# GpSimd casting loads for w_ch1, TensorE row broadcasts and a two-ring DMA model in a hand-planned attention and mixer kernel

## The chip, the cores and the metric

The kernel runs on one core of a Trainium2 chip. The metric is device time in microseconds (us): the median of five runs.

## The reference

Sliding-window attention with sinks over q, k, v of shape (4, 8, 768, 64) is followed by a residual mixer MLP over 512 features. All inputs and the output are float32.

```python
# attention, n_sink = 4, window = 128
scores = q @ k.T / sqrt(64)
keep = (pos_k < 4) | ((0 <= pos_q - pos_k) & (pos_q - pos_k < 128))
x = softmax(where(keep, scores, -1e9)) @ v          # -> (4, 768, 512)
# mixer
a1 = alpha1 * x + beta1
u = x + lam * einsum('ts,bsd->btd', w_tok, a1)       # w_tok 768 x 768
a2 = alpha2 * u + beta2
out = u + lam * (relu(a2 @ w_ch1) @ w_ch2)           # 512 x 2048, 2048 x 512
```

## The kernel before

All four batches (b = 0 to 3) run in one program. Every step is registered as a task with `add` (L51): a priority, the engines that could run it with a cost in ns for each, the function that emits the instruction, the tasks it comes after, the buffers it uses. `Plan.emit` (L63) is a list scheduler: it always takes the task that could start earliest by its own clock, and of those that tie the one with the lowest priority number; it chooses engine and buffer and emits the instruction. So the order in every engine's queue, SyncE's DMA queue among them, follows from the costs written into the source. A DMA lands in the planner's clock after one shared `channel` (L129 to L131): issue, 1600 ns, then the transfers one after the other by their `lands`. Buffers are named by kind with a fixed number of homes (L211): eight "nat" (q or k of a head pair), four "wst" (staging of 512 KB weight pieces), four "d" (one PSUM bank each), two "S" (two PSUM banks each).

Per batch: q and k are loaded in fp32, cast to fp16 (`n16`), transposed to `qkT` (batches 0 and 1 on TensorE with the tile `tp`, L431; later ones by DMA transposes, L445). `scores` (L500) multiplies them into `S`, ScalarE takes the exponential into `E` (L538), VectorE masks it (L547) or a bias matmul did (L518). `pv` (L555) multiplies by v (`vf`) and normalises into `x` (L593, L594). For batch 0 GpSimd multiplies each half of x by lam*alpha1 (`la1_b`) into `xh` (L603); for later batches it multiplies and adds lam*beta1 (`lb1_b`; L612, L615). `tok` (L692) is the token matmul with the transposed w_tok (`wtokT`), added to x (L710), giving u. u is cast (L226 or L228), transposed (batch 0 on TensorE, L745; later by DMA, L763), scaled (`affine`, L725), and goes through `mlp1` (h, L784, relu L790 or L792) and `mlp2` (ch, L808, added at L819, stored at L822). Work on batch b + 1's attention is planned among batch b's MLP.

What the change touches:

- w_ch1 (`load_w1`, L391): eight loads of 512 KB by SyncE into "wst" staging, then sixteen casts (`cast_w1`, L669) on ScalarE, GpSimd or VectorE into `w1f`. w_ch2 uses the same staging (`load_w2`, L396) and is multiplied by lam while it is cast (`cast_w2`, L678, into `w2f`).
- lam, alpha1, beta1: three one-partition rows are loaded by ScalarE's queue (L240). `spread` (L662) broadcasts a row over 128 partitions with an fp32 matmul by a row of ones; before, only lam*alpha1 goes that way. lam and beta1 are also loaded again by SyncE with a broadcast (`load_const`, L386, 256 KB each), and GpSimd multiplies them at full size (L859). A row of lam*beta1 in fp16 (`lb16`) serves batch 0's extra token matmul (L705).
- row sums of w_tok (`row`, L646): six matmuls per tile of `wtokT` by a matrix with one column of ones.
- idle matmuls (L217, L112): where the planner's TensorE has a gap before 14 us of its clock, it emits one 128-column matmul per 75 ns of gap, into one PSUM bank that is held back for it until 14.5 us (L215, L222).
- v of batch 0 (`cast_v0`, L628) goes to GpSimd or ScalarE.

Of the kernel before, what the change touches and what calls it, by code (L numbers as in the profile page):

```python
# [12 lines left out]

PE, ACT, DVE, POOL, SP = "pe", "act", "dve", "pool", "sp"
# [4 lines left out]
class Buf:  # L19


    def __init__(self, kind, shape, dtype, name):
        self.kind, self.shape, self.dtype, self.name = kind, shape, dtype, name
        self.left = 0
        self.freed = 0.0
        self.home = None
        self.t = None

# [11 lines left out]
class Plan:  # L40
# [10 lines left out]
    def add(self, prio, engs, fn, after=(), uses=(), mode=None, lands=0.0, port=False,  # L51
            since=0.0):

        t = Task(prio, engs, fn, after, uses, mode, lands, port)
        t.ready = max(t.ready, since)
        for b in uses:
            b.left += 1
        for a in t.needs:
            a.then.append(t)
        self.tasks.append(t)  # L60
        return t

    def emit(self):  # L63
# [3 lines left out]
        open_ = []  # L67

# [3 lines left out]
        for t in self.tasks:  # L72
            if not waiting[id(t)]:
                admit(t)
        free = {e: 0.0 for e in (PE, ACT, DVE, POOL, SP)}
        mode = None
        channel = 0.0
        port = 0.0
        done = 0
        while done < len(self.tasks):  # L80
# [20 lines left out]
            assert best is not None, "no task can go on"  # L101
# [11 lines left out]
            if e == PE and free[PE] < until:  # L113
                for _ in range(int((start - max(free[PE], 900.0)) / took)):
                    idle()
                    mode = None
            t.fn(e)
            cost = t.engs[e]
            if e == PE:
                if start < 4500.0:  # L120
                    cost = cost * 2
                if t.mode != mode:
                    cost = cost + 95
                mode = t.mode
# [4 lines left out]
            if e == SP:  # L129
                channel = max(channel, free[e] + 1600.0) + t.lands  # L130
                t.seen = channel + 300.0  # L131
            else:
                t.seen = free[e] + SEEN[e]
            for b in t.uses:
                b.left -= 1
                b.freed = max(b.freed, t.seen)
                if b.left == 0:
                    self.busy[b.kind][b.home] = False
                    self.homes[b.kind][b.home] = b.freed
            for o in t.then:  # L140
                o.ready = max(o.ready, t.seen)
                waiting[id(o)] -= 1
                if not waiting[id(o)]:
                    admit(o)
            done += 1
# [4 lines left out]
def kernel(  # L150
# [64 lines left out]
    idle_ps = ps.tile([P, 512], FP32, tag="d_3", bufs=1, name="idle")  # L215

    def idle():  # L217
        nc.tensor.matmul(idle_ps[:, 0:P], iden, iden, start=True, stop=True)

    plan = Plan(pools, homes, (14000.0, idle, 75.0))  # L220
    add = plan.add
    plan.homes["d"][3] = 14500.0  # L222
# [33 lines left out]
    ones_c = const.tile([P, P], FP16, name="ones_c")  # L256
    nc.vector.memset(ones_c, 0.0)
    nc.vector.memset(ones_c[:, 0:1], 1.0)
# [60 lines left out]


# [10 lines left out]
    def load_qk(p, b, hp, t, wait=None):  # L331
        bf = nat[b, hp, t] = Buf("nat", None, None, f"nat{b}_{hp}_{t}")
        src = (q, k)[t][b, 2 * hp : 2 * hp + 2]
        if b < XB:
            src = src.rearrange("h (p r) d -> p h (r d)", p=P)
            done["nat", b, hp, t] = add(
                p, {SP: 480}, lambda e: nc.sync.dma_start(bf.t, src), [wait], [bf], lands=1110)  # L337
        else:
            src = src.rearrange("h s d -> (h s) d").rearrange("(x p) d -> p x d", p=P)
            done["nat", b, hp, t] = add(  # L340
                p, {SP: 700}, lambda e: nc.sync.dma_start(
                    bf.t.rearrange("p e (r d) -> p (e r) d", r=NR), src), [wait], [bf], lands=1740)

    def load_v(p, b, r, wait=None):
        bf = vn[b, r] = Buf("vnat", None, None, f"vnat{b}_{r}")
        done["vn", b, r] = add(
            p, {SP: 550}, lambda e: nc.sync.dma_start(
                bf.t, v[b, :, r * P : (r + 1) * P, :].rearrange("h p d -> p h d")),
            [wait], [bf], lands=1150)
# [3 lines left out]
    def load_v0(p, G, r):  # L353
        if G == 0:
            if r == 0:
                v0[G, 0] = Buf("uT", [P, NR, 4, D], FP32, "v0_0")
            bf, sl = v0[G, 0], r
        else:
            if r % 3 == 0:
                v0[G, r // 3] = Buf("wst", [P, 3, 4, D], FP32, f"v0_1_{r // 3}")  # L360
            bf, sl = v0[G, r // 3], r % 3
        v0["at", G, r] = (bf, sl)
        done["v0", G, r] = add(
            p, {SP: 520}, lambda e: nc.sync.dma_start(  # L364
                bf.t[:, sl], v[0, 4 * G : 4 * G + 4, r * P : (r + 1) * P, :].rearrange("h p d -> p h d")),
            uses=[bf], lands=590)
# [3 lines left out]
    def load_wtok(p, ti):  # L370
        if ti % 3 == 0:
# [5 lines left out]
            uses=[bf], lands=1060)  # L377
# [3 lines left out]
    def load_w(p, key, src):  # L381
        bf = wst[key] = Buf("wst", None, None, f"wst_{key}")
        done["wst", key] = add(
            p, {SP: 400}, lambda e: nc.sync.dma_start(bf.t, src), uses=[bf], lands=1400)

    def load_const(p, name, tile_, src):  # L386
        done[name] = add(
            p, {SP: 500}, lambda e: nc.sync.dma_start(tile_, src.unsqueeze(0).to_broadcast([P, DM])),
            lands=850)

    def load_w1(p, i):  # L391
        for c in range(0, NC, 2):
            load_w(p + 0.1 * c, f"w1_{i}_{c}",
                   moe_w_ch1[c * P : (c + 2) * P, i * 512 : (i + 1) * 512].rearrange("(c p) f -> p c f", p=P))
# [16 lines left out]
    def trans(p, b, hp, t, engs, evac, cast_p=None, wait=None):  # L411
# [31 lines left out]
        if b >= XB:  # L443
# [4 lines left out]
                [a] + prior, [bn, o], lands=600)  # L448
# [179 lines left out]
    def cast_v0(p, G, r):  # L628
        bf, sl = v0["at", G, r]
        done["vf", 0, r, G] = add(  # L630
            p, ({POOL: 400, ACT: 408}, {POOL: 400})[G],
# [4 lines left out]
    def cast_wtok(p, ti):  # L636
# [3 lines left out]
        pr = Buf("d", [P, P], FP32, f"rs{ti}")  # L640

# [3 lines left out]

        def row(e):  # L646
            for si in range(NR):
                nc.tensor.matmul(
                    pr.t, ones_c, wtokT[:, si, ti * P : (ti + 1) * P],
                    start=(si == 0), stop=(si == NR - 1))  # L650

        a = add(p, {ACT: 831, POOL: 829}, lambda e: copy(e, w.t.rearrange("p r i -> p (r i)"), src.t[:, ti % 3, :]),
                [done["wtn", ti]], [src, w], port=True)
        a = add(p + 0.1, {PE: 330}, tr, [a], [w, pt])
# [3 lines left out]
        a = add(p + 0.3, {PE: 330}, row, [a], [pr])  # L658
# [3 lines left out]
    def spread(p, name, src, o):  # L662
# [3 lines left out]
                [done.get(name)], [pt], since=9000.0)  # L666
        done[name] = add(p + 0.1, {DVE: 600, ACT: 600}, lambda e: copy(e, o, pt.t), [a], [pt])

    def cast_w1(p, i):  # L669
        for c in range(NC):  # L670
            src = wst[f"w1_{i}_{c - c % 2}"]
            done["w1", i, c] = add(
                p, {ACT: 619, POOL: 618, DVE: 430},
                lambda e, c=c, src=src: copy(
                    e, w1f[:, c, i * 512 : (i + 1) * 512], src.t[:, c % 2, :]),
                [done["wst", f"w1_{i}_{c - c % 2}"]], [src], port=True)
# [80 lines left out]
    def uTx(p, b, ti):  # L757

        if (b, 0) not in uT:
# [5 lines left out]
            [done["u16", b, ti]], [bu, bo], lands=600)  # L765
# [3 lines left out]
        for c in range(NC):  # L769
            o = (c, slice(chk * NTOK, (chk + 1) * NTOK))  # L770
            done["uT", b, chk, c] = add(
                p + 0.1 + 0.01 * c, {DVE: 380, ACT: 500},
# [3 lines left out]
    def mlp1(p, b, chk, fi):  # L776
# [11 lines left out]
        def relu(e):  # L788
            if e == ACT:
                nc.scalar.activation(bh.t[:, fi, :], ph.t, AF.Relu)  # L790
            else:
# [3 lines left out]
                [done["uT", b, chk, c] for c in range(NC)] + [done["w1", fi // 4, c] for c in range(NC)],  # L795
# [3 lines left out]
    def mlp2(p, b, ti, part):  # L799
# [16 lines left out]
        if part == 3:  # L816
            def oa(e):
# [6 lines left out]
                [a], [bx], lands=800)  # L824


    t0 = -1000.0
    n = 0
# [17 lines left out]
    load_w1(at(), 0)  # L846
    load_const(at(), "lam", lam_b, moe_lam)
    load_const(t0 + 150, "b1", lb1_b, moe_beta1)
    for i in range(1, 4):
        load_w1(at(), i)  # L850

    def spread_rows():
        done["la1"] = add(-880, {POOL: 1270}, lambda e: nc.gpsimd.tensor_mul(rows[1], rows[1], rows[0]),
                          since=9000.0)
        spread(-879, "la1", rows[1], la1_b)
        a = add(-990, {POOL: 400}, lambda e: nc.gpsimd.memset(lb16.t, 0.0), [], [lb16])
        done["lb1"] = add(-879, {POOL: 1270}, lambda e: nc.gpsimd.tensor_mul(lb16.t[0:1], rows[2], rows[0]),
                          [a], [lb16], since=9000.0)
        done["lb1b"] = add(20, {POOL: 1270}, lambda e: nc.gpsimd.tensor_mul(lb1_b, lb1_b, lam_b),  # L859
                           [done["lam"], done["b1"]])  # L860
        pt = Buf("d", [P, 2 * NC], FP32, "abT")
        a = add(-850, {PE: 200}, lambda e: nc.tensor.transpose(pt.t, ab_row, iden8), [], [pt],
                since=9000.0)
# [12 lines left out]
    for G in range(2):  # L876
        base = -900 + 60 * G
        for j in range(NR):
            scores(base + 10 * j, 0, j, (G,), bias=G == 1 or j > 1)
# [6 lines left out]
    cast_w1(1.5, 0)  # L886
# [5 lines left out]
    for b in range(B):  # L892
# [17 lines left out]
        if b == 0:  # L910
            for i in range(1, 4):
                cast_w1(w0 + 8 + 8 * (i - 1) - 4, i)
# [13 lines left out]
        if b + 1 < B:  # L926
            nb = b + 1
            if nb >= XB:
                for i, (hp, t) in enumerate(QK_ORDER):
                    load_qk(w0 - 30 + i, nb, hp, t, done["qkT", b, 3, 1])  # L930
                for r in range(NR):
                    load_v(w0 - 20 + r, nb, r, done["qkT", b, 3, 1])
# [8 lines left out]
            for i, (what, *args) in enumerate(steps):  # L941
                p = w0 + lo + (hi - lo) * i / len(steps) + 0.5
                if what == "T":
                    hp, t = QK_ORDER[args[0]]
                    trans(p if nb < XB else w0 - 15 + i, nb, hp, t, {POOL: 829}, {DVE: 955, ACT: 800},
# [47 lines left out]
```

The softmax here doesn't subtract the row's maximum and nothing guards it: scores larger than these inputs give would overflow.

## Time and profile before

| | us |
|---|---|
| median of 5 runs | 274.21 |
| lowest, highest | 272.13, 276.47 |
| the profiled execution | 272.13 |
| its span | 270.4 |
| TensorE busy (share of the span) | 258.3 (96%) |
| VectorE, ScalarE, GpSimd busy | 142.7, 129.9, 116.5 |
| first batch-0 h matmul | 43.12 |
| last w2f multiply ends | 82.5 |

The span is what the profiler recorded of one execution, and all shares refer to it. TensorE's matmuls are pipelined and their ends are modelled: a 128-column matmul is shown with 219 ns although such matmuls follow each other much more closely, so a busy TensorE need not be at its peak, and a gap shorter than such an end is not shown. The granted TensorE clock is 1.00 in this run from start to end. "Idle before, releaser" names what an instruction waited for last.

### The profile page before, as it was taken

The numbers are of one execution on the slowest core, as the hardware profiler recorded it, in microseconds if no ns is written. First come the engines' busy times: TensorE is split into PE (matmuls) and PEld (weight loads), VectorE is DVE, ScalarE is ACT, GpSimd is POOL, SyncE is SP. The second block draws the span as 40 slices with busy tenths as digits, with TensorE's granted clock in tenths as the row PEclk, the third lists the DMA queues.
The fourth block names the chain that finished last, engine by engine and source line by source line (L and its number), as shares of the span: only waits on it lengthen the run. The fifth ranks groups of instructions, "written<-read, shape, count | busy, mean of one in ns | idle before, by whom it ended". The sixth has DMA issues, their size and how long they took to land.

```text
span 270.4 us, 4969 instructions
## 1 busy us (share of the span) xinstructions
PE 258.3 (96%) x1941; PEld 141.6 (52%) x1941; DVE 142.7 (53%) x292; ACT 129.9 (48%) x213; POOL 116.5 (43%) x139
## 2 busy tenths in 40 slices
PE   7889999997899999799999999999999999999994
PEld 7544746654454544356655444555654445565441
DVE  5465745678899925357884234378953343100222
ACT  2688836777842003789640025787600145773000
POOL 5579947820596793117988600005755000000000
PEclk9999999999999999999999999999999999999999
DMA  6999998999999736799967523200011232000222
GB/s 208 322 247 354 383 312 252 293 350 282 235 282 204 190 92 168 175 190 215 217 136 164 153 78 97 62 0 2 0 39 44 97 98 80 0 0 2 78 78 78
DMA packets 85838, 42.28 MB, mean 156 GB/s; under 512 B 73515, under 2 KB 77619, under 8 KB 85814
## 3 DMA queue, kind: packets, MB, share of 16 engines
q1 hardware_dynamic: 85792, 41.95, 58.0%
q8 instruction: 15, 0.25, 0.4%
q14 instruction: 9, 0.07, 0.1%
q10 hardware_dynamic: 22, 0.01, 0.0%
HBM read 30.16 MB, written 6.29 MB: 135 GB/s over the span
## 4 chain that ended last, share of the span: by engine, by line
PE 68%; DMA 16%; SPq 5%; DVE 5%; POOL 2%; issue 1%; ACT 1%; DVEq 0%; POOLq 0%; ACTq 0%
PE ch L808 29%; PE h L784 24%; PE tok L701 9%; DMA wst_w<-in_moe_w_ch_dram 8%; DMA nat<-in_q_dram 6%; SPq L364 3%; DMA lb_b<-in_moe_beta_dram 3%; DVE w2f L683 3%; PE pv L570 3%; PE S L523 2%; DVE E L547 1%; SPq L375 1%; PE pv L563 1%; POOL n L228 1%; SPq L337 1%
## 5 line engine op out<-in xcount | busy, mean ns | idle before, releaser
L784 PE MATMUL h<-uT,w1f 128*128 128x384 f16 x512 | 90.3, 326 | 2.9 <-DVE uT L730 1.5
L808 PE MATMUL ch<-w2f,hT 128*128 128x512 f16 x384 | 88.5, 379 | 0.2 <-DVE w2f L683 0.2
L784 PEld LDWEIGHTS <-w1f 128*128 128x128 f16 x512 | 47.7, 98 | 36.2 <-issue 7.1
L808 PEld LDWEIGHTS <-hT 128*128 128x128 f16 x384 | 36.3, 98 | 41.4 <-issue 0.9
L790 ACT ACTIVATE hT<-h 128x384 f16<-128x384 f32 x95 | 46.2, 493 | 18.7 <-PE h L784 17.0
L538 ACT ACTIVATE E<-S 128x1024 f16<-128x1024 f32 (+1 forms) x42 | 40.7, 1002 | 12.9 <-PE pv L570 8.2
L819 DVE TENSOR_TENSOR x<-x,ch 128x512 f32<-128x512 f32 x24 | 16.5, 686 | 52.2 <-PE ch L808 51.7
L612 POOL TENSOR_TENSOR tmp<-x,la_b 128x512 f32<-128x512 f32 x18 | 25.8, 1435 | 41.4 <-DVE x L594 39.1
L226 ACT CAST u<-x 128x512 f16<-128x512 f32 x20 | 12.3, 618 | 61.7 <-DVE x L710 61.7
L701 PE MATMUL tok<-xh,wtokT 128*128 128x512 f16 x144 | 34.4, 379 | 0.0
L228 POOL CAST n<-nat 128x768 f16<-128x768 f32 x28 | 25.9, 937 | 16.7 <-DMA nat<-in_q_dram 11.9
L710 DVE TENSOR_TENSOR x<-x,tok 128x512 f32<-128x512 f32 x24 | 16.4, 687 | 23.6 <-PE tok L701 18.6
L615 POOL TENSOR_TENSOR xh<-tmp,lb_b 128x512 f16<-128x512 f32 x18 | 25.4, 1414 | 0.7
L792 DVE TENSOR_SCALAR hT<-h 128x384 f16<-128x384 f32 x33 | 18.3, 554 | 10.6 <-PE h L784 10.3
L547 DVE TENSOR_TENSOR E<-E,maskn 128x1024 f16<-128x1024 f16 x25 | 23.7, 977 | 0.0
L701 PEld LDWEIGHTS <-wtokT 128*128 128x128 f16 x144 | 13.9, 98 | 16.1
L594 DVE TENSOR_TENSOR x<-pv,rec 128x256 f32<-128x256 f32 x48 | 20.4, 424 | 1.7
L570 PE MATMUL pv<-vf,E 128*128 128x65 f16 x328 | 18.1, 194 | 2.3 <-DVE E L547 1.1
L570 PEld LDWEIGHTS <-E 128*128 128x128 f16 x328 | 15.3, 97 | 8.4 <-DVE E L547 1.8
L228 POOL CAST vf<-vnat 128x512 f16<-128x512 f32 x18 | 10.8, 618 | 9.3 <-PE h L784 7.1
L683 DVE TENSOR_TENSOR w2f<-wst_w,lam_b 128x512 f16<-128x512 f32 x15 | 12.6, 878 | 3.5 <-DMA wst_w<-in_moe_w_ch_dram 3.5
L228 POOL CAST u<-x 128x512 f16<-128x512 f32 x4 | 2.5, 629 | 26.3 <-DVE x L710 26.3
(94 smaller groups left out, 202.5 us busy)
## 6 DMA issues: line engine op xcount, KB each, us to landing
wst_w<-in_moe_w_ch_dram SPq DMA_DIRECT2D x16, 512.0 KB, 7.5
nat<-in_q_dram SPq DMA_DIRECT2D x16, 384.0 KB, 5.7
nat<-in_k_dram SPq DMA_DIRECT2D x16, 384.0 KB, 8.2
out_dram<-x SPq DMA_DIRECT2D x24, 256.0 KB, 2.0
vnat<-in_v_dram SPq DMA_DIRECT2D x18, 256.0 KB, 5.2
wtn<-in_moe_w_tok_dram SPq DMA_DIRECT2D x6, 384.0 KB, 5.6
v<-in_v_dram SPq DMA_DIRECT2D x12, 128.0 KB, 4.9
uT<-u SPq DMA_TRANSPOSE x18, 2.3
```

The costliest lines, as they stand in the source:

```text
L228: engine[e].tensor_copy(o, i)
L538: nc.scalar.activation(eT.t, pS.t[:, :, 0 : n * w].rearrange("p e (i w) -> p e i w", i=n), AF.Exp, scale=scale)
L547: nc.vector.tensor_mul(ev, ev, m.to_broadcast(list(ev.shape)))
L570: nc.tensor.matmul(po.t[:, hl, :], eT.t[:, e_, off + i, c : c + P], vf[j][:, h, :], start=(r < 2 and n == 0), stop=(n == len(parts) - 1 an ...
L594: nc.vector.tensor_mul(bx.t[:, 4 * G : 4 * G + 4, :], po.t[:, :, 0:D], rec.t.to_broadcast([P, 4, D]))
L612: nc.gpsimd.tensor_mul(tmp.t, bx.t.rearrange("p h d -> p (h d)"), la1_b)
L615: nc.gpsimd.tensor_add(bh.t, tmp.t, lb1_b)
L683: lambda e, a=a, src=src: engine[e].tensor_mul(w2f[:, a, :], src.t[:, a % 2, :], lam_b),
L701: nc.tensor.matmul(pt.t, wtokT[:, si, ti * P : (ti + 1) * P], hs[si].t, start=(si == 0), stop=(si == NR - 1 and b > 0))
L784: nc.tensor.matmul(ph.t, w1f[:, c, fi * P : (fi + 1) * P], bu.t[:, c, chk * NTOK : (chk + 1) * NTOK], start=(c == 0), stop=(c == NC - 1))
L790: nc.scalar.activation(bh.t[:, fi, :], ph.t, AF.Relu)
L808: nc.tensor.matmul(pc.t, bh.t[:, fi, nt * P : (nt + 1) * P], w2f[:, fi, :], start=(fi == 0), stop=(fi == NF - 1))
```

## The change

The planner gets a class `Rings`: two rings, "hw" for SyncE's transfers and "sw" for GpSimd's, each transfer with a number of packets and ns per packet (`lands` is now such a pair). While both have work, a packet of each goes in turn. SyncE's issue takes longer in the planner's clock when its ring holds more than 128 packets, or when the transfer eight before it hasn't landed. Tasks that wait for a transfer are released at its modelled landing. Then:

- w_ch1 is loaded by four GpSimd DMAs of 1 MB (2 KB runs) that cast to fp16 on the way, straight into `w1f`, from 20 us of the planner's clock; no staging, no casts.
- lam and lam*beta1 are broadcast by `spread` too; the two broadcast loads and the full-size multiply go; the row work may start at 5.5 us instead of 9.
- w_tok's cast is only on ScalarE and gives the row sum through its accumulator; a copy puts it in a column of `rcol`, and one matmul by the identity makes the row.
- idle matmuls are emitted up to 36 us of the planner's clock, into whichever "d" bank is free; no bank is held back.
- Batch 0's v casts may also go to VectorE, later q and k casts also to ScalarE; the q/k and v loads of batches 2 and 3 get later priorities; the `affine` of later batches is priced 700 instead of 500 ns on ScalarE. `BIAS` gives the same choice as before.

```diff
+IDLE = 36000.0
+class Rings:
+    WIRE = {"hw": 1600.0, "sw": 1900.0}
+    HOLDS = 128.0
+    def room(self, ring, lands, at):
...
+        last = g[-8] if len(g) >= 8 and g[-8].seen is None else None
...
+        while ring == "hw" and over > 0 and q:
...
+    def step(self, until):
...
+            turn = sum(h[2] for r, h in live)
+            ends = [(self.now + h[1] * turn, r) for r, h in live]
...
             until, idle, took = self.fill
-            if e == PE and free[PE] < until:
-                for _ in range(int((start - max(free[PE], 900.0)) / took)):
-                    idle()
+            n = int((start - max(free[PE], 900.0)) / took)
+            if e == PE and free[PE] < until and n > 0:
+                free_d = [(h, i) for i, (h, x) in enumerate(zip(self.homes["d"], self.busy["d"])) if not x]
+                if free_d and min(free_d)[0] < free[PE]:
+                    h = min(free_d)[1]
+                    idle(self.pools["d"][0].tile(
+                        [P_, 512], FP32, tag=f"d_{h}", bufs=1, name=f"idle{done}"), n)
+                    self.homes["d"][h] = start
                     mode = None
...
+            if t.lands:
+                cost += rings.room("sw" if e == POOL else "hw", t.lands, start) - start
...
-    plan.homes["d"][3] = 14500.0
...
+    rcol = const.tile([P, S // P, P], FP16, name="rcol")
+    nc.vector.memset(rcol, 0.0)
...
     def load_w1(p, i):
-        for c in range(0, NC, 2):
-            load_w(p + 0.1 * c, f"w1_{i}_{c}",
-                   moe_w_ch1[c * P : (c + 2) * P, i * 512 : (i + 1) * 512].rearrange("(c p) f -> p c f", p=P))
+        done["w1", i] = add(
+            p, {POOL: 760}, lambda e: nc.gpsimd.dma_start(
+                w1f[:, :, i * 512 : (i + 1) * 512],
+                moe_w_ch1[:, i * 512 : (i + 1) * 512].rearrange("(c p) f -> p c f", p=P)),
+            lands=(32, 96), since=W1_SINCE)
...
-            p, ({POOL: 400, ACT: 408}, {POOL: 400})[G],
+            p, {POOL: 400, ACT: 408, DVE: 330},
...
+        def cast(e):
+            nc.scalar.activation(
+                w.t.rearrange("p r i -> p (r i)"), src.t[:, ti % 3, :], AF.Copy, accum_out=col.t)
+        def mid(e):
+            nc.vector.tensor_copy(rcol[:, ti, 0:1], col.t)
         def row(e):
-            for si in range(NR):
-                nc.tensor.matmul(
-                    pr.t, ones_c, wtokT[:, si, ti * P : (ti + 1) * P],
-                    start=(si == 0), stop=(si == NR - 1))
+            nc.tensor.matmul(pr.t, rcol[:, ti, :], iden, start=True, stop=True)
...
-    load_const(at(), "lam", lam_b, moe_lam)
-    load_const(t0 + 150, "b1", lb1_b, moe_beta1)
+    load_w1(-770, 0)
     for i in range(1, 4):
-        load_w1(at(), i)
+        load_w1(-769, i)
...
+        a = done["lb1b"] = add(-878, {POOL: 1270}, lambda e: nc.gpsimd.tensor_mul(rows[2], rows[2], rows[0]),
+                               since=ROWS)
+        z = add(-990, {POOL: 400}, lambda e: nc.gpsimd.memset(lb16.t, 0.0), [], [lb16])
+        done["lb1"] = add(-876, {ACT: 600, DVE: 600}, lambda e: copy(e, lb16.t[0:1], rows[2]),
+                          [z, a], [lb16])
         spread(-879, "la1", rows[1], la1_b)
...
-        done["lb1b"] = add(20, {POOL: 1270}, lambda e: nc.gpsimd.tensor_mul(lb1_b, lb1_b, lam_b),
-                           [done["lam"], done["b1"]])
+        spread(SPREAD, "lb1b", rows[2], lb1_b)
+        spread(SPREAD + 1, "lam", rows[0], lam_b)
...
-                    load_qk(w0 - 30 + i, nb, hp, t, done["qkT", b, 3, 1])
+                    load_qk(w0 + i, nb, hp, t, done["qkT", b, 3, 1])
...
-                    load_v(w0 - 20 + r, nb, r, done["qkT", b, 3, 1])
+                    load_v(w0 + 10 + r, nb, r, done["qkT", b, 3, 1])
...
```

## The prediction, as it was made before the result was known

> **What bounds the kernel now.** I read the page first: engine totals, the slices, the chain.
>
> ```profile
> PE 258.3 (96%) x1941; PEld 141.6 (52%) x1941; DVE 142.7 (53%) x292; ACT 129.9 (48%) x213; POOL 116.5 (43%) x139
> ...
> DVE  5465745678899925357884234378953343100222
> ...
> DMA  6999998999999736799967523200011232000222
> ...
> PE 68%; DMA 16%; SPq 5%; DVE 5%; POOL 2%; issue 1%; ACT 1%; DVEq 0%; POOLq 0%; ACTq 0%
> ```
>
> TensorE is occupied nearly throughout, and from about 83 us the chain is TensorE alone. Its non-TensorE part (DMA 16%, SP 5%, VectorE 5%) lies in the first 80 us, where the DMA row is full and the VectorE row rises to 9. So I cut the span at the work's own boundaries (columns: stretch, its length, busy us of PE, PEld, DVE, ACT, POOL, clock, DMA share, GB/s).
>
> ```profile
> 0.00:14.60 14.60, 12.14 (x133) 9.38 (x133) 6.96 (x27) 7.11 (x8) 8.52 (x23) 1.00 0.90 263
> 14.60:43.12 28.52, 27.61 (x298) 15.65 (x298) 17.89 (x45) 20.33 (x31) 21.67 (x34) 1.00 1.00 312
> 43.12:58.92 15.80, 15.05 (x130) 9.98 (x129) 9.40 (x17) 11.34 (x23) 10.35 (x17) 1.00 1.04 328
> 58.92:83.00 24.08, 21.68 (x181) 11.44 (x181) 21.78 (x36) 16.04 (x25) 9.99 (x7) 1.00 1.13 262
> 83.00:100.50 17.50, 17.50 (x126) 8.95 (x125) 11.62 (x24) 1.02 (x1) 15.22 (x13) 1.00 0.64 152
> 100.50:111.20 10.70, 8.99 (x41) 3.91 (x40) 6.13 (x11) 4.92 (x8) 4.02 (x7) 1.00 0.75 182
> 111.20:167.86 56.66, 56.64 (x406) 30.11 (x406) 30.55 (x62) 26.61 (x44) 29.82 (x28) 1.00 0.71 157
> ```
>
> Up to 14.6 us TensorE mostly runs fillers (83 "idle" matmuls). After 111 us it has no gap except the last add and store: nothing is to be won there. TensorE gaps: 0.91 before 43.12, 0.75 to 58.92, 2.40 to 83 (VectorE 21.78 of 24.08), 1.71 before 111.2; 5.8 us together. [...]counting each start-to-start distance against the dense rate of its shape, I get 4.6 us in 58.92 to 83 and 2.2 in 100.5 to 111.2[...]. What ended the gaps (TensorE's timeline; start, us, then idle before and its releaser):
>
> ```profile
> 65.09 0.30 PE L570 MATMUL pv<-vf,E 128*128 128x65 f16 x4 [1.13 <-DVE E L547]
> ...
> 71.93 1.46 PE L784 MATMUL h<-uT,w1f 128*128 128x384 f16 x8 [0.68 <-DVE hT L792]
> ...
> 110.21 7.18 PE L784 MATMUL h<-uT,w1f 128*128 128x384 f16 x40 [1.52 <-DVE uT L730]
> ```
>
> VectorE is late because w2 is late. SyncE's waits (us in all, times, longest) show w2's loads (L384, the line for w1 too) held by staging buffers that w1's casts had not freed; SyncE's queue shows the last of them mixed with batch 2's q and k.
>
> ```profile
> SPq L384 <- ACT w1f L226: 4.3, 3, 3.2
> ...
> SPq L384 <- POOL w1f L228: 3.6, 2, 3.3
> ```
>
> ```profile
> 47.23 10.68 SPq L384 DMA_DIRECT2D wst_w<-in_moe_w_ch_dram x6
> 57.95 0.47 SPq L341 DMA_DIRECT2D nat<-in_q_dram  x1
> ...
> 65.91 3.67 SPq L384 DMA_DIRECT2D wst_w<-in_moe_w_ch_dram  x1
> ...
> 72.16 2.13 SPq L384 DMA_DIRECT2D wst_w<-in_moe_w_ch_dram  x1
> ```
>
> All 16 w2f multiplies (15 on VectorE, 0.88 us mean, 13.2 in all) thus fall at 58.3 to 82.6 us, amid batch 1's masks and norms. Batch 1's xh on GpSimd ends only at 98.6, its 36 token matmuls stand in one block at 100.5, and the MLP waits at 108.5 for u, its DMA transpose and uT.
>
> [...] The granted clock here is 1.00 in every stretch, so fillers up to 36 us have no clock to win.
>
> **Part by part** (minus is shorter).
>
> w1. Removed: 8 SyncE loads, and 16 casts, 8 on ScalarE and 8 on GpSimd at 0.62 us (5.0 us each); the four wst buffers go to w2 alone. Added: four 1 MB GpSimd DMAs. Bytes stay the same: from the trace's packets (2 KB 93 ns, 1.5 KB 72, 3 KB 137, 256 B 19.7, per engine) everything through w2 without batch 2 needs q/k 9.2, v 7.6, w_tok 6.6, w1 11.9, q/k 9.2, v 7.6, w2 11.9 = 64 us from 1.9, so about 66, against about 80 now with 15 us of batch-2 q/k mixed in. w2's rank is ahead of those; it lacked buffers. The last w2f multiply moves from 82.5 to about 70, the first from 58 to about 40, into VectorE's free 6.4 us of 43 to 59 and the 10.6 before. I take 2.5 us out of 58.92 to 83 (page gap 2.4, dense count 4.0; bounds 0 and 4). Before 58.92 the gaps end at qkT copies, behind w1f casts on ScalarE: 0.5 (0 to 0.75). With batch 1's attention earlier its tokens can stand among the ch matmuls, as they already do for batches 2 and 3 in the chain; I take 1.5 of 1.71 (0 to 2.2). Together -4.5. First w1 use is 43.1; issued from 20 us at half rate a 1 MB piece takes 6 us, so they land near 28, 34, 40, 46, before the uses: hidden by a few us at least; a piece that is later than its use costs TensorE each us of that.
>
> GpSimd's issue. Behind each DMA stand xh multiplies (0.73 us each, 12), whose last at 33.5 releases the token block of 9 us. No such issue is in the trace; the planner puts in 0.76; [...]I take 4 x 0.9 = 3.6. Taken away from GpSimd before 33 us: two w_tok casts 1.65 and two w1f casts 1.24; several of its eleven v casts of 0.4 may go to VectorE. Net 0.
>
> Rows. Two broadcast loads go (0.5 MB, 1.5 us of ring, and 1.27 us of GpSimd at 40.9). Two fp32 spreads come at 1.05 us (b_la at 13.58, the next at 14.63) with two evacuations of 0.69 on VectorE. They are free from 5.5 us, where fillers stand: nothing; +2.1 if they fall among scores.
>
> Row sums. 36 matmuls at about 0.07 us (12 in 0.89 at 28.8) = 2.5 us become six at 0.08: -2.0 of TensorE, but the token block waits for xh on GpSimd, not for these; I count -0.5 (0 to -2). Six tiny copies (0.17) on VectorE; all w_tok casts on ScalarE with the sum, 0.85 us, two more than now against two w1f casts fewer: nothing while ScalarE keeps its gaps of 30 to 35 us, 0.4 if it doesn't.
>
> Fillers. Up to 36 us by the planner's clock, one per 75 ns of planned gap, about 65 ns on the chip (11 in 0.71 us at 9.84). A planned gap that the chip doesn't have is lost: +0.5 (0 to 3). They now rotate over the four d banks; before, one bank was held back till 14.5.
>
> Ring model, later loads of batches 2 and 3, transposes' choice of engine, affine 700: no work, order alone. TensorE is dense after 111 us and hides it; a late SyncE transpose would cost that whole wait. Zero (-0.5 to +2).
>
> Sum: -4.5 + 0 + 0 - 0.5 + 0.5 = -4.5. The profiled execution took 272.13 (span 270.4, 1.7 around it): 267.6. It was the fastest of five; against the median 274.21 the same ratio gives 269.7.
>
> **Rivals.**
> A, the forecast, 269.7; 0.50, own range 267 to 271.4.
> B, more comes free: also the rest of the dense-count gaps and 2 us of the token block (POOL's casts gone): -9, so 265. For: GpSimd and ScalarE shed 10 us before 60. Against: TensorE had only 0.9 us of page gap before 43. 0.12.
> C, given back: w2 still waits (SyncE is held by w1's ring share till about 46), VectorE stays the bound at 59 to 83, and the row-sum gain pays the fillers: 274; 0.20. For: the ring was full throughout.
> D, slower: [...]From 1.85 us each ((4.5+2.9)/4) it eats the gain. Against: v casts can leave GpSimd[...]. 0.18.
>
> A difference under 1% (2.7 us) can hardly be told from none here. Faster by over 1% (below 271.5): A nearly whole and B, 0.59; same 0.22; slower by over 1% 0.19. Eight in ten: 264 (B with its bound) to 277 (C and the nearer half of D).
>
> **What would show it.** Right: w2f multiplies from about 40 and done by 72; no VectorE-released gaps over 0.5 us at 59 to 83; batch 1's tok matmuls in pieces among ch; no wait near 108; first h near 43. Wrong: first h after 45, long DMA issues on GpSimd before 33, w2f still near 80, or TensorE gaps after 111.

## The result, and the profile after

The change is worth next to nothing: 273.15 us (median of 43 runs, 270.46 to 275.64) against 273.57 for the kernel before (80 runs, 271.32 to 276.82), a ratio of 0.9981 with a 95% interval of 0.9965 to 0.9997. The forecast was 1.6% faster (269.7 against the 274.21 known then). Medians are of all runs, and ratios compare the means of those runs that lie within 1.5% of the fastest of their kernel. The profiled execution of the changed kernel took 274.07 us with a span of 272.4. It lies 0.9 above its median, while the profiled one of before lay 1.4 below its own, so of the 2.0 us between the two spans most is chance; what counts is where inside the spans the time moved.

The page of the changed kernel, first the rows that answer to those of before:

```profile
PE 258.2 (95%) x1844; PEld 137.8 (51%) x1844; DVE 144.1 (53%) x299; ACT 134.8 (49%) x222; POOL 109.8 (40%) x124
...
DVE  4367655498798745525896245279853344000222
...
DMA  6999999839944999499909898200011234000221
...
PE 89%; DVE 4%; DMA 4%; issue 1%; ACTq 0%; ACT 0%; SPq 0%; DVEq 0%
```

TensorE has 97 instructions fewer and is as busy as before (258.2 against 258.3): the same time for less work. The stretches that answer to those of before, cut at this kernel's own boundaries (first S 15.58, first h 45.94, batch 1's tokens 99.65, end of the wait 111.25; 60 to 83 stands for 58.92 to 83; columns as in the prediction):

```profile
0.00:15.58 15.58, 9.95 (x39) 4.89 (x39) 6.45 (x25) 5.37 (x9) 10.38 (x23) 1.00 0.91 259
15.58:45.94 30.36, 29.64 (x296) 16.01 (x296) 19.79 (x53) 22.99 (x39) 19.28 (x31) 1.00 1.08 317
...
60.00:83.00 23.00, 22.30 (x182) 11.87 (x181) 20.38 (x32) 16.05 (x24) 15.30 (x12) 1.00 0.81 184
...
99.65:111.25 11.60, 8.58 (x45) 3.73 (x44) 6.08 (x10) 5.63 (x10) 1.39 (x2) 1.00 0.86 192
```

In 60 to 83 us TensorE's page gap is 0.70 where 58.92 to 83 had 2.40: the middle did improve. The first stretch holds 39 matmuls where it held 133, and ends later. The last one has a gap of 3.02 instead of 1.71. By marks (before, after, in us of each span): first h 43.1, 45.9; from there to the last ch of batch 0 57.2, 53.5; from there to the second batch's first h 9.9, 12.1; from there to the last ch 156.0, 156.5. So +2.8, -3.7, +2.2, +0.5. TensorE's timeline of the changed kernel shows the two losses (columns as before):

```profile
4.67 0.82 PE L521 MATMUL tp<-iden,n 128*128 128x128 f16 x6 [4.67 <-POOL iden L386]
...
7.73 0.24 PE L949 MATMUL abT<-iden,ab_row 8*128 8x8 f32 x1 [0.95 <-DMA ab_row<-in_moe_beta_dram]
7.85 2.04 PE L759 MATMUL b_lam<-row,ones_r 1*128 1x512 f32 x2
...
13.64 2.07 PE L759 MATMUL b_lb1b<-row,ones_r 1*128 1x512 f32 x2
15.65 1.04 PE L612 MATMUL S<-qkT 64*128 64x256 f16 x8
...
111.25 0.28 PE L612 MATMUL S<-qkT 64*128 64x256 f16 x2 [3.02 <-DMA qkT<-n]
111.46 8.36 PE L869 MATMUL h<-uT,w1f 128*128 128x384 f16 x40
```

And the kernel before at its start:

```profile
1.43 4.37 PE L218 MATMUL idle<-iden 128*128 128x128 f16 x42 [1.43 <-POOL iden L248]
5.63 0.50 PE L432 MATMUL tp<-iden,n 128*128 128x128 f16 x6
...
10.55 0.66 PE L523 MATMUL S<-qkT 64*128 64x256 f16 x8
```

Before, 42 fillers stand ahead of the first transposes, and six transposes take 0.50 us. After, no filler stands there, six transposes take 0.82, and eight S matmuls take 1.04 instead of 0.66. At 18.41 us two bias matmuls still take 1.06; at 20.12 they take 0.59. So the array runs at half rate until about 19.5 us, while the window row says clock 1.00 for 0 to 15.58. The clock records in the traces begin only at 19.5 us here and at 5.3 us in the kernel before, and the column counts the time without a record as full: at the start it doesn't report the clock, and the length of a known instruction does. The clock of 1.00 "from start to end" given above for the kernel before is known only from 5.3 us on. Below, full rate means that such instructions take their short length, and half rate that they take about twice that.

Two lines of the diff explain the missing fillers. The planner's TensorE is free at 0 and all banks are free at 0, so `min(free_d)[0] < free[PE]` asks whether 0 < 0, and the first gap gets no filler. The changed kernel emits 12 idle matmuls instead of 83.

### The profile page after: what moved, and what is told of

Read it like the earlier page. It is cut to its first block, busy times and chain, and to the rows that moved or that the text cites. A ratio compares the mean times of both kernels' runs of the same rounds, so it can differ in the third digit from the quotient of the medians.

```text
span 272.4 us, 4769 instructions
## 1 busy us (share of the span) xinstructions
PE 258.2 (95%) x1844; PEld 137.8 (51%) x1844; DVE 144.1 (53%) x299; ACT 134.8 (49%) x222; POOL 109.8 (40%) x124
## 4 chain that ended last, share of the span: by engine, by line
PE 89%; DVE 4%; DMA 4%; issue 1%; ACTq 0%; ACT 0%; SPq 0%; DVEq 0%
PE ch L893 31%; PE h L869 30%; PE tok L786 10%; PE S L612 4%; PE pv L659 4%; PE tp L521 2%; DMA ab_row<-in_moe_beta_dram 2%; DVE w2f L768 2%; PE S L607 2%; PE pv L652 1%; DMA qkT<-n 1%; DMA uT<-u 1%; PE b_lb1b L759 1%; PE b_la L759 1%; PE b_lam L759 1%; DVE qkT L317 1%
## 5 line engine op out<-in xcount | busy, mean ns | idle before, releaser
L869 PE MATMUL h<-uT,w1f 128*128 128x384 f16 x512 | 91.9, 330 | 0.8 <-DVE hT L877 0.7
L875 ACT ACTIVATE hT<-h 128x384 f16<-128x384 f32 x90 | 44.2, 492 | 25.2 <-PE h L869 25.0
L315 ACT CAST u<-x 128x512 f16<-128x512 f32 x18 | 11.1, 618 | 42.8 <-DVE x L795 42.0
L877 DVE TENSOR_SCALAR hT<-h 128x384 f16<-128x384 f32 x38 | 21.0, 555 | 18.7 <-PE h L869 18.1
L704 POOL TENSOR_TENSOR xh<-tmp,lb_b 128x512 f16<-128x512 f32 x18 | 24.6, 1365 | 1.3
L317 POOL CAST vf<-vnat 128x512 f16<-128x512 f32 x18 | 12.8, 717 | 28.3 <-DMA vnat<-in_v_dram 26.7
L636 DVE TENSOR_TENSOR E<-E,maskn 128x1024 f16<-128x1024 f16 x25 | 23.0, 948 | 0.0
L317 POOL CAST n<-nat 128x768 f16<-128x768 f32 x15 | 12.7, 863 | 12.0 <-DMA nat<-in_q_dram 5.1
L612 PE MATMUL S<-qkT 64*128 64x256 f16 (+1 forms) x168 | 14.1, 277 | 3.0 <-DMA qkT<-n 3.0
L315 ACT CAST n<-nat 128x768 f16<-128x768 f32 x13 | 10.6, 832 | 9.5 <-DMA nat<-in_q_dram 7.0
```

What stands on the lines that cost most here:

```text
L315: nc.scalar.copy(o, i)
L317: engine[e].tensor_copy(o, i)
L612: nc.tensor.matmul(pv_[:, e_, i, :], o.t[rows, 2 * hp + 1, j * P : (j + 1) * P], o.t[rows, 2 * hp, j * P : j * P + w], start=not bias, sto ...
L636: nc.vector.tensor_mul(ev, ev, m.to_broadcast(list(ev.shape)))
L704: nc.gpsimd.tensor_add(bh.t, tmp.t, lb1_b)
L869: nc.tensor.matmul(ph.t, w1f[:, c, fi * P : (fi + 1) * P], bu.t[:, c, chk * NTOK : (chk + 1) * NTOK], start=(c == 0), stop=(c == NC - 1))
```

## Experiments

A time is a median, beside the kernel before, which ran again each time on the same chip (273.5 to 273.9); ratios are to before.

**The first fillers.** Put back in the changed kernel:

```diff
-                if free_d and min(free_d)[0] < free[PE]:
+                if free_d and min(free_d)[0] <= free[PE]:
```

> The changed kernel with one comparison relaxed, so that the fillers before the first transpose are emitted again (43 idle matmuls). Theory F (the array runs at half rate until about 19 us because nothing ran on it before the first transpose): six transposes shown with 0.50 us instead of 0.82, a row broadcast 1.05 instead of 2.0 us, first h near 43.5 instead of 45.9, time 2 to 2.5 us below the changed kernel, some 270.8, ratio to before 0.990. Rival R (the first 20 us are long because three broadcasts and a wait for the alpha2/beta2 rows stand in TensorE's queue): first h after 45, less than 0.7 us gained.

270.77 us, ratio 0.989 [0.9849, 0.993]: 0.9% under the changed kernel (0.989 / 0.9981), some 2.5 us. First h at 43.7. Its timeline:

```profile
1.44 4.77 PE L308 MATMUL idle<-iden 128*128 128x128 f16 x43 [1.44 <-POOL iden L337]
...
8.81 1.12 PE L759 MATMUL b_la<-row,ones_r 1*128 1x512 f32 x2
...
11.57 2.07 PE L759 MATMUL b_lb1b<-row,ones_r 1*128 1x512 f32 x2
13.58 1.04 PE L612 MATMUL S<-qkT 64*128 64x256 f16 x8
```

The array is at full rate at 8.81 (a spread takes 1.12) and at half rate again at 11.57 (2.07). The converse, the kernel before without the fillers of its first gap:

> The kernel before without its 42 idle matmuls ahead of the first transpose. Theory F: half rate well past 10 us, first h 1.5 to 3 us later than 43.1, time 1.5 to 3 us longer, ratio 1.006 to 1.011. Rival R: first transpose about 1 us earlier (4.7 instead of 5.6 us), time within 0.5 us of before.

275.31 us, ratio 1.0047 [1.0021, 1.0072], first h 44.5: the same sign, +1.3 us, less than expected. Other fillers and no row of spreads follow there, and the rate is full from 9.6 us. Its profile also has a wait of 1.51 us for v before 13.16 that the kernel before doesn't have, so how much of the 1.3 is the rate stays open.

**The spreads.** The changed kernel with the spreads of lam and lam\*beta1 from 24 us of the planner's clock and abT from 9 us, without and with the first fillers:

```diff
-        spread(SPREAD, "lb1b", rows[2], lb1_b)
-        spread(SPREAD + 1, "lam", rows[0], lam_b)
+        spread(SPREAD, "lb1b", rows[2], lb1_b, 24000.0)   # new argument: since
+        spread(SPREAD + 1, "lam", rows[0], lam_b, 24000.0)
```

> The kernel after, still without first fillers; the spreads of lam and lam*beta1 moved to 24 us of the planner's clock, the products of the bias to 9 us. Theory C ([...]the spreads keep the array at half rate until 19.5 us): full rate begins by 10 to 13 us, the first scores S by 12.5, first h at 43.5, time 270.5 to 272. Rival (only the missing fillers count): full rate begins at 16 or later, S first at 12.5 all the same because two spreads at 2.05 us are no longer ahead of it, first h at 44.5 to 45, time 272 to 273.

> Fillers at the first gap and late spreads together. Theory C: full rate from 7 us and no half-rate stretch at 10 to 17 us, S first by 11, first h at 41.5 to 42.5 (against 43.7 with the fillers alone), time 268.5 to 269.5. Rival (the spreads only cost their own length): the half-rate stretch at 10 to 17 us stays, first h at 43, time 270 to 271.

late_spreads: 269.78 us, ratio 0.9822 [0.9783, 0.9861]. Theory C missed here: in its profile S starts at 13.1, but half rate lasts to 19.9 us; the spread of lam\*alpha1 still stands at 9.3 to 11.3. That profiled execution took 272.8, well over its median, so its marks don't explain the gain. fill_late: 268.12 us, ratio 0.9763 [0.9729, 0.9798], the lowest median of all; first S at 10.5, no half rate at 10 to 17 us. But first h came at 42.8, not before 42.5: 1.5 us behind the two moved spreads (26.48 to 28.4 us) a new half-rate stretch begins, the clock of 30 to 35 us being 0.67.

Side by side, against the changed kernel and by ratio: the fillers alone are worth 2.5 us, the later spreads alone 4.3, both 6.0 (by the medians 2.4, 3.4 and 5.0). The two gains don't add up, and with six runs each the intervals can't tell which of the two is larger. The moves also change what the planner does afterwards, so these are not gains of the first 20 us alone.

Whether the half rate comes with the one-row matmul as such needed the same order with another operand ("one-row" because the row of ones and the row to be spread lie in one partition: the trace lists the matmul as 1\*128 by 1x512). The kernels from here on whose names begin with t_ have TensorE transposes in place of DMA transposes, and are compared with each other. t_late is fill_late so changed, t_first is fill_first:

> fill_late with all of its DMA transposes (q and k of batches 2 and 3, u of batches 1 to 3) replaced by TensorE transposes as the first batches have them; it is the base of the runs that follow, whose names begin with t_. All theories: first 43 us as in fill_late (first S at 10.5, first h at 42.8, a half-rate stretch of 3.4 us behind the two adjacent spreads or none[...]). TensorE gets 16 x 6 + 18 x 4 = 168 more transposes at 0.056 us, 9.4 us in all, and the waits for SyncE's transposes before 108 us go: 273 to 277 us.

> fill_first (the change with its first fillers, spreads as the change has them) on TensorE transposes alone. All theories: the half-rate stretch at 10.3 to 17.1 us as in fill_first, first S at 13.6, first h 43.7; time 2 to 3 us above t_late.

t_late: 275.89 us, ratio 1.0074 [1.0051, 1.0097]. t_first: 277.16, ratio 1.0117 [1.0059, 1.0175]. In t_full_rows only the operands differ from t_first. Theory C puts the half rate down to the one-row operands, the rival to the gaps at 7 to 12 us or to fp32 as such:

```diff
-    rows = [sb.tile([1, DM], FP32, ...
+    rows = [sb.tile([P, DM], FP32, ...          # zeroed, the row in partition 0
-    ones_r = const.tile([1, P], FP32, name="ones_r")
+    ones_r = const.tile([P, P], FP32, name="ones_r")
```

> t_first with the three rows and the row of ones as tiles of 128 partitions (rows 1 to 127 of the data zero, of the ones 1.0): the spreads keep their place and length, but their matmuls use all 128 rows of the array. Theory C [...]: no half-rate stretch at 10 to 17 us, the spread of lam*beta1 1.05 instead of 2.07 us, first S at 11 to 11.5, first h at 42 to 42.7, time 1 to 1.5 us under t_first. Rival [...]: the half-rate stretch stays, first S at 13 to 14, time as t_first.

275.92 us, ratio 1.0082 [1.005, 1.0115]; first h 41.8 against t_first's 43.5. Stretches of t_first (the clock is the third column from the end):

```profile
10.00:12.50 2.50, 2.50 (x15) 1.37 (x15) 2.10 (x4) 2.08 (x5) 1.07 (x2) 0.59 1.07 363
12.50:15.00 2.50, 2.50 (x16) 0.95 (x15) 0.69 (x1) 1.27 (x2) 1.51 (x3) 0.50 1.13 235
15.00:17.50 2.50, 2.50 (x19) 1.27 (x18) 2.04 (x3) 1.17 (x3) 2.15 (x5) 0.54 0.81 177
```

and of t_full_rows:

```profile
10.00:12.50 2.50, 2.50 (x18) 1.23 (x17) 2.33 (x4) 1.51 (x3) 1.47 (x3) 1.00 0.99 331
12.50:15.00 2.50, 2.50 (x29) 1.31 (x28) 2.22 (x5) 2.33 (x6) 1.45 (x3) 1.00 1.19 254
15.00:17.50 2.50, 2.50 (x30) 1.29 (x28) 2.50 (x5) 2.50 (x5) 2.37 (x5) 1.00 0.81 166
```

With the spreads in the same places, as long (the first two 1.12 and 1.08 us against 1.10 and 1.12) and as fp32, but with operands of 128 partitions (128\*128 by 128x512), the half-rate stretch is gone (clock 1.00 at 10 to 17.5 us against 0.50 to 0.59), in spite of a wait of 0.98 us at 8.7 that t_first doesn't have. The other executions agree with the two profiles: the mean clock of all six of t_first is 0.979 to 0.990, that of all 14 of t_full_rows 0.993 to 1.00. So between these two kernels the clock followed the operands, as theory C had it; the times (1.2 us apart, intervals overlapping) agree but couldn't show it alone. First S came at 12.7, not 11.5, behind that wait. The two late spreads moved apart were planned but not measured.

**w_ch1.** The kernel before with w_ch1 by four GpSimd casting DMAs, nothing else:

> The kernel before with w_ch1 alone moved to four GpSimd casting loads (no staging, no casts, old DMA model with both issuers in one line, fillers as before). My forecast's step: w2f multiplies start near 40 us and end by 72, VectorE-released gaps at 59 to 83 us go, time 2.5 to 4.5 us below before, ratio 0.985 to 0.991. Rival G (staging wasn't what held w2; multiplies still end near 80): within 1 us of before.

279.48 us, ratio 1.0227 [1.0179, 1.0275]: slower. The first w2f multiply is at 42.3, but the old one-channel model now orders batch 1's casts wrongly: TensorE waits 6.05 us for an n cast before 54.36, and first h falls to 60.0. So the run shows what the loads cost under the old model's order, and doesn't judge the loads themselves. The other way round, t_late with w_ch1 through staging and casts again:

> t_late with w_ch1 as before the change: eight SyncE loads of 512 KB into staging and sixteen casts, under the new two-ring model. Theory W1 (the 3.7 us that the change won between first h and the end of batch 0's ch come from w_ch1's casts and staging being gone): w2f from 58 to 83 us with most multiplies on VectorE, TensorE gaps of 4 to 6 us at 43 to 83 again, time 3 to 4 us above t_late. Rival (they come from the model and the orders alone): time within 1 us of t_late.

279.44 us, ratio 1.0228 [1.0173, 1.0283], 3.55 us over t_late, as theory W1 said, though w2f runs from 50.1 to 79.8 and not later than in the changed kernel. Where TensorE loses it in t_w1 (busy of PE and of DVE are the first and third numbers behind the length):

```profile
54.00:60.00 6.00, 6.00 (x48) 3.42 (x47) 6.00 (x8) 4.90 (x9) 4.36 (x4) 1.00 0.95 242
60.00:66.00 6.00, 4.98 (x46) 2.69 (x43) 6.00 (x7) 5.19 (x9) 4.20 (x4) 1.00 1.11 331
66.00:70.00 4.00, 1.95 (x17) 1.00 (x18) 3.03 (x7) 0.67 (x2) 3.95 (x4) 0.86 1.05 380
70.00:74.00 4.00, 4.00 (x35) 2.29 (x32) 2.09 (x6) 2.40 (x4) 3.48 (x3) 0.71 1.08 360
```

and in t_late:

```profile
60.00:66.00 6.00, 6.00 (x50) 3.34 (x49) 4.52 (x8) 4.46 (x7) 2.96 (x4) 1.00 1.03 297
66.00:70.00 4.00, 3.95 (x44) 2.33 (x43) 3.90 (x11) 3.52 (x6) 0.60 (x1) 1.00 1.05 369
```

VectorE is full for 12 us, TensorE waits (3.07 us of page gap at 60 to 70, against 0.05), and behind the wait the array runs at half rate for another 3.4 us (68.9 to 72.3; clock 0.86 and 0.71 in the two rows).

**w_ch2 and the priorities.** The changed kernel with the old priorities of the loads of batches 2 and 3:

> The changed kernel with the priorities of the later q, k and v loads put back to those of before. Theory P (the 3.0 us wait of batch 2's scores at 108 us comes from q and k loads of batch 2 issued as late as 100 us): the wait goes, time 2 us below the changed kernel, 271.2. Rival: the token block of batch 1 still stands in one piece ahead of its MLP, so a wait of 1.5 to 2 us for u and its transposes takes its place: gain 1 us or less.

273.28 us, ratio 0.998 [0.996, 1.0]: as the changed kernel. The wait of 3.02 us for qkT and its half-rate stretch are gone, one of 1.52 us for uT stands there instead, as in the kernel before (second batch's first h 109.2 against 111.5), but TensorE's gaps, an estimate counted from the traces against the dense rate, are 3.1 instead of 1.4 us at 112 to 168. Half of theory P was right. On top of fill_late, w_ch1's four loads spaced, and then the old priorities as well:

> As fill_late, and the four w_ch1 loads of GpSimd spaced at 20, 30, 38 and 46 us of the planner's clock instead of all at 20. Theory W (w_ch1 in one go takes half of the DMA engines, so w_ch2 cannot land before 50): the first w2f multiply at 45 to 48, the last by 78, VectorE's late multiplies at 79 to 82 gone, time 1 us under fill_late. Rival (the ring is full either way and only the order changes): w2f still ends at 81 to 83, time within 0.5 us of fill_late; if a w_ch1 piece becomes late for its h, TensorE waits for w1f at 44 to 60 and the time is 1 to 3 us above.

> As fill_late_spaced, with the priorities of the q, k and v loads of batches 2 and 3 as before. Theory P (the later priorities make the wait of 3.0 us before 111 us and the half-rate stretch behind it): no wait over 1 us at 100 to 112, no half rate there, 1 to 2 us under fill_late_spaced. Rival (as in old_prio the gain is lost again in gaps at 121 to 146): the second wait of h falls but batch 1's MLP takes 59 instead of 57.5 to 58 us, time within 0.5 us of fill_late_spaced.

269.55 us, ratio 0.9814 [0.978, 0.9847], and 270.66 us, ratio 0.9872 [0.9842, 0.9903]. Spacing brings the w2f multiplies forward (47.7 to 76.7 against 49.4 to 78.8) and wins nothing: TensorE's counted gaps at 43 to 83 are 3.7 against 2.0, and the last ch comes at 261.7 against 261.6. With the old priorities the time rises again (the intervals just overlap), so they weren't the better choice either.

**The small terms.** t_late with six row-sum matmuls per tile, and t_late with `IDLE` at 14 us:

> t_late with the row sums of w_tok by six matmuls per tile, as before the change, and no accumulator on ScalarE's cast. The prediction priced the new row sums at -0.5 us (0 to -2): then first h is 0.5 us later than t_late's 41.5 and the time 276.4. Rival 1 (TensorE is dense from 26 to 43 us once its clock is full, so all of the 30 matmuls saved count): first h at 43.5, time 278. Rival 2 (ScalarE's longer casts, 0.84 + 0.2 instead of 0.83 us, cost what the matmuls save): first h within 0.3 us of 41.5, time within 0.5 us of t_late.

> t_late with fillers only up to 14 us of the planner's clock instead of 36; five or six idle matmuls fewer. The prediction priced the later fillers at +0.5 us (0 to 3): then 275.4. Rival 1 (they are too few to cost: t_late has 0.2 us of them after 20 us): the same within 0.3 us. Rival 2 [...]: half-rate stretches between 14 and 40 us and 1 to 2 us more.

276.49 us, ratio 1.0079 [1.0048, 1.011], and 275.3 us, ratio 1.0044 [1.0024, 1.0065]. The profiled execution of t_six_sums lay 3.4 us over its median, so its first h isn't compared. Against t_late (1.0074) the row sums move the time by +0.1 and dropping the later fillers by -0.8 us. Both have the forecast's sign and size within what these intervals can tell, which isn't much. That the later fillers keep the array at full rate has no support: 6 of 22 executions of t_idle14 have a mean clock of at least 0.997, against 2 of 22 of t_late. (The profile of t_idle14 has a half-rate stretch at 11.9 to 15.3 us; that of t_late, taken in its fastest execution, has none.) Neither term holds the missing 4 us.

## Why the prediction was wrong, step by step

**Fillers: the first step that failed.** The prediction said that "fillers up to 36 us have no clock to win", since "The granted clock here is 1.00 in every stretch", and put +0.5 us. It took a column without a record for a record of full speed, and it read the diff's condition without trying it at time zero. With the first fillers the array is at full rate early: from 5.3 us on in the kernel before (9.6 in before_no_first_fill), from 6.9 us in fill_first (19.5 in the changed kernel), by the transposes of 0.50 against 0.82 us. Without them the change lost about 2.5 us (fill_first).

**Rows: the second.** "They are free from 5.5 us, where fillers stand: nothing; +2.1 if they fall among scores." All three stood ahead of the first S, behind a wait of 0.95 us for ab_row, at some 2.05 us each instead of 1.05; and with them the array fell back to half rate where it had been at full rate (t_first against t_full_rows: clock 0.50 to 0.59 against 1.00 at 10 to 17.5 us, and 1.7 us at first h). Moving two of them away was worth 1.2 us in the pair without DMA transposes (1.0117 to 1.0074, intervals overlapping) and 3.5 in the other (0.989 to 0.9763; 2.7 by the medians), in whose profiles fill_first has a half-rate stretch at 109.3 to 112.7 that fill_late escapes. That the upper bound of +2.1 lies among these is luck: it was the spreads' own length, and their effect on the rate was not in it.

**The middle: right in size, for half of its reason.** Forecast were -2.5 at 59 to 83 (its dense count there, 4.6 us, was taken as 4.0 by an estimate of the author's); the marks give -3.7 from first h to the end of ch, and t_w1 gives 3.55 for w_ch1's path alone, its half-rate stretch included. But w2f didn't run "from about 40" and wasn't "done by 72": it ran from 52.5 to 82.6 us. GpSimd's queue in the changed kernel, with its DMA issues:

```profile
29.24 0.94 POOL L480 DMA_DIRECT2D w1f<-in_moe_w_ch_dram  x1
...
49.38 3.16 POOL L317 CAST n<-nat 128x768 f16<-128x768 f32 x4 [1.79 <-PE tp L521]
52.51 3.73 POOL L768 TENSOR_TENSOR w2f<-wst_w,lam_b 128x512 f16<-128x512 f32 x3
```

The first w2f waits for no DMA: it stands behind four casts, where the planner's clock put it. The four staging buffers were filled by loads issued at 28.3 to 31.9, which landed at most 15.1 us later, so by 47; SyncE then stood still until the buffers came free:

```profile
SPq L476 <- DVE w2f L768: 17.8, 4, 12.6
```

The DMA row of 26 to 60 us (40 slices of 0.85 us) shows the rings run dry at 53 to 57:

```profile
DMA  9999999999999999999999999999999400000378
```

So staging still held w_ch2 up; the buffers, no longer shared with w_ch1, were waiting for the planner. What helped, as far as it is shown, was that staging and the sixteen casts were gone: t_w1 puts them back, still with eight multiplies on GpSimd (nine in t_late), and loses the 3.55 us. That seven multiplies went to GpSimd instead of one, so that VectorE keeps nine of 1.10 us where it had fifteen of 0.88, may have helped too, but no run tested it. The stretch to 83 us has 0.70 us of gap. The prediction's other sign, no VectorE-released gap over 0.5, was missed by one of 0.70 us at 64.97.

**The wait at 108: the sign was wrong.** Forecast -1.5, since batch 1's tokens were to stand among ch; they stand in one block again at 99.65, and the wait before 111.25 became 3.02 us, now for the transposed k of batch 2, which SyncE issues at 108.44 behind three transposes of u. The step that failed is "Ring model, later loads of batches 2 and 3 ...: no work, order alone", put at "Zero (-0.5 to +2)". Its own bound of +2 for a late SyncE transpose is what came. And behind that wait, too, the array runs at half rate: the clock is 0.68 at 111 to 113 and 0.50 at 113 to 115, and the first twelve h take 3.8 us to the end of the last, where twelve at 45.88 us take 2.1. A single stretch of 3.4 us at half rate in a span of 272.4 makes a mean clock of 0.994, and 32 of the 44 executions of the changed kernel have at most that, against 42 of 117 of the kernel before; where in the kernel the stretch lay is known for the profiled ones alone.

**What held.** GpSimd's issues took 0.75 to 0.94 us (forecast 0.9), so rival D, with issues of 1.85 us and more, is out (that length was the author's estimate; none was shown); no h waited for w_ch1; row sums and later fillers were small. The case that came is the rival "given back", at its 274, but not by its mechanism (ring share and fillers): the gain of the middle was made and was given back by a slower array at the front and by the wait at 108. With both faults of the front mended (fill_late) the kernel runs in 268.1 us, below the forecast of 269.7; that doesn't confirm the forecast's sum, whose parts came out otherwise.

## What to carry to other kernels

Look for the array's real rate in the length of a known matmul (here six transposes, 0.50 or 0.82 us), above all at the start of a kernel, before calling fillers there useless. Try a changed guard at its first case: here one `<` at time zero cost as much as half of the planned gain. A wait (3.02 us before 111.25 in the changed kernel) or a run of one-row matmuls (26.48 to 28.4 us in fill_late) on TensorE cost its own length here and then a half-rate stretch of 3.4 us behind it, though not each of them did; price both.

## What the runs showed of the hardware

- Behind one-row fp32 matmuls (1 x 128 by 1 x 512) a half-rate stretch stood in fill_first (10.3 to 17.1 us), t_first (10.5 to 17.3) and fill_late (29.9 to 33.3); with operands of 128 partitions in t_full_rows there was none (clock 1.00 at 5 to 55 us). In t_late's profile the same pair of late spreads left the clock at 1.00, but that is one of two such executions: the other 20 of 22 have a mean clock of at most 0.994.
- The same wait has different sequels: 3.02 us before 111.25 (changed kernel) and 1.75 before 108.25 (fill_first) were followed by half rate (clock 0.61 at 112 to 116, 0.66 at 108 to 112), 1.91 before 106.59 (fill_late) was not (1.00 at 108 to 116). No run was made to show what decides it.
- What goes with such a stretch in time: in the largest set of runs 26 executions of the kernel before with a mean clock of at least 0.998 averaged 273.4 us, and 17 with at most 0.994 averaged 274.6, so 1.2 us; the other three sets give 0.7, 1.4 and 1.8.
- A casting 1 MB load by GpSimd landed 11.7 to 17.0 us after its issue in the changed kernel. At 34 to 50 us, while SyncE's ring had work too, the trace has 1846 packets of GpSimd's ring and 1842 of SyncE's. Until 43.5 us each ring takes about half of the busy time (0.57 and 0.55 of the 16 engines). The packets of the four loads run from 33.7 to 52.6 us, 3.6 to 5.5 us a load, where the prediction has 6.
